# Other places for the last raw weight pieces, an earlier first layer, and VectorE alone for the inverse's copy and the turns of the state

## The chip, the cores and the metric

One core of a Trainium2 chip. The metric is the device time of one execution in microseconds (us). A run is the median of some executions. Ratios are the mean time of one kernel's fast runs over the mean time of the other's fast runs of the same rounds, so they are not quite the ratio of the medians that are quoted beside them. "Faster" or "slower" needs 2%.

One profile is one execution, and profiles scatter.

## The reference

Two layers one behind the other: a linear recurrence over 768 steps for 4 x 8 heads of width 40, then a feed-forward block on its output.

```python
def _attn_ref(r, k, v, w, a, b):              # each (4, 8, 768, 40)
    state = np.zeros((B, H, D, D))
    for t in range(S):
        y[:, :, t] = np.einsum('bhd,bhde->bhe', rt, state)
        Sa = np.einsum('bhde,bhe->bhd', state, at)
        state_decay = state * wt[:, :, None, :] - np.einsum('bhd,bhe->bhde', Sa, bt)
        state = state_decay + np.einsum('bhd,bhe->bhde', vt, kt)

def _moe_ref(x, w_in, w_out):                 # x (3072, 320), w_in (320, 2048), w_out (2048, 320)
    h = x @ w_in
    g = h * (1.0 / (1.0 + np.exp(-h)))
    return (g @ w_out)
```

The weights come as raw 64-bit numbers and are turned into fp32 on the chip.

## The kernel before

The recurrence runs in 12 chunks of 64 steps. A chunk needs the inverse of a triangular matrix per head. VectorE computes the inverses row by row (31 rows for a pair of chunks; for chunks 0 to 3 only 15 rows of half the size, and TensorE completes them with small products, `corners` and `complete`, in the "merge"). The inverse goes through DRAM (`mi`, `xd`, `XT`) to change its layout. From chunk 4 on, everything comes in pairs of chunks.

The feed-forward block of two finished chunks is cut into steps that fill TensorE's gaps: first-layer steps F (`ph`, then Silu on ScalarE into `gts`) and output steps S (`po<-wo_s,gts`, 16 matmul records each). Steps keep their order among themselves; against everything else the framework orders the queue of each engine by when it expects things to be ready, unless an order is laid down with `behind`. Each engine works its queue in order.

The raw weights arrive in pieces. A piece waits for a free place, is loaded there, and is converted by five VectorE and three ScalarE operations:

```python
def load_weights(done):
    while len(rooms) < NW:
        n = len(rooms)
        if n < NW // 2:
            place = ("wi0", "wi1", "wo0", "wo1", "room")[n % 5]
        elif n < NW * 3 // 4:
            place = ("wo0", "wo1", "room")[(n - NW // 2) % 3]
        else:
            place = ("mi", "tmp", "room")[(n - NW // 2) % 3]
        if taken.get(place, -1) > done:
            return
        ...

def weights(n, pin=lambda x: x, more=True):     # first half of piece n, second half of piece n-1
    if n < NW:
        pin(nc.vector.tensor_scalar(out=e, in0=hi, ...)); pin(nc.vector.tensor_scalar(out=f, in0=hi, ...))
        nc.scalar.activation(out=e, ...); nc.scalar.activation(out=f, ...); nc.scalar.activation(out=lo, ...)
    ...
    pin(nc.vector.scalar_tensor_tensor(...)); pin(nc.vector.tensor_tensor(...))
    pin(nc.vector.tensor_tensor(out=pieces[n][0], in0=f, in1=e, op=ALU.mult))
    if more: load_weights(n)

def in_order(x, line="moe"):                    # keeps the F and S steps in order
    if line in issued: behind(x, issued[line])
    issued[line] = x.ins
...
box["qq"] = sb.tile([128, N, 48], F32, name="qq", tag="tmp" if n > 0 else "xt")   # in merge()
...
def back():                                     # end of an inverse
    turned = XI.rearrange("p t s -> p s t")
    nc.scalar.copy(out=mi[L, 0:16], in_=turned[L, 0:16])
    pin(nc.vector.tensor_copy(out=mi[L, 16:32], in_=turned[L, 16:32]))
    send(queue, xd[L], mi[L])
...
for n in range(2, 4):                           # chunks 2 and 3
    ...
    now = {2: 4, 3: 5}[n]
    x = prepare(n + 2)
    if n == 2:
        weave(steps[0:4], queue[0:1], [x[i] for i in (0, 5, 1, 6)], convert[31:34])
    ...
    weave(steps[4:6] + late.pop(n, []) + ..., queue[1:now], scores + rows[0:36],
          convert[34:] if n == 2 else [])
```

## Time and profile before

901.05 us. In the profile (span 899.2 us) I use these places in time. They are read from the order of time on VectorE and TensorE. In the lines of profiles PE is TensorE's matmuls, PEld its weight loads, DVE VectorE, ACT ScalarE, POOL GpSimd and SPq the queue in which SyncE issues transfers; L825 is line 825 of that kernel. "Cold" means a granted TensorE clock of 0.50, "warm" one of 1.00.

| us from the start | kernel before |
|---|---|
| rows of the inverse of chunks 2 and 3 | 193.1 to 205.6 |
| qq of the merge of chunk 2, of chunk 3 | 220.6, 247.2 |
| first row of chunk 5 (inverse of chunks 4 and 5) | 310.0 |
| end of the rows of chunks 5, 7, 9, 11 | 349.3, 474.3, 597.8, 720.2 |
| the three later pairs together | 370.9 |
| last row to the end ("tail") | 179.0 |

Read it as three sums: the front up to the rows of chunk 5, three pairs, the tail. A change is worth what it does to each of the three.

### The profile page before, as it was taken

How to read it: one execution, taken by the hardware profiler on the slowest of the kernel's cores; microseconds unless marked ns; L12 is line 12 of the kernel's file. 1: busy time of each engine (PE TensorE's matmuls, PEld its weight loads, DVE VectorE, ACT ScalarE, POOL GpSimd, SP SyncE). 2: the span in 40 equal slices, each digit the busy share in tenths (PEclk: the TensorE clock that was granted, in tenths of full speed). 3: DMA queues.
4: the chain of work that ended last, by engine and by line, in shares of the span. 5: the costliest groups of instructions: out<-in, count | busy, mean ns of one | idle time of the engine just before them, and what ended most of it. 6: DMA issues, size and time to landing. Idle time of an engine off the chain costs nothing.

```text
span 899.2 us, 25358 instructions
## 1 busy us (share of the span) xinstructions
PE 778.9 (87%) x10914; PEld 552.9 (61%) x10914; DVE 557.9 (62%) x1084; ACT 297.4 (33%) x689; POOL 151.4 (17%) x156
## 2 busy tenths in 40 slices
PE   2145689896898997999998999999999989999995
PEld 2135677674786853875746857648757468574643
DVE  9979889885439598176896295982768912510000
ACT  2234358532622322514025342226140243311120
POOL 7312024200202201303102240113031000000001
PEclk9999869996759998999999999999999999999998
DMA  7875646744325542444613627325424021102001
GB/s 154 167 147 142 150 130 150 166 106 107 90 59 128 105 110 47 115 108 87 145 34 62 157 64 158 93 48 117 96 56 122 16 61 40 42 23 57 1 1 33
DMA packets 240151, 82.99 MB, mean 92 GB/s; under 512 B 207136, under 2 KB 231968, under 8 KB 240032
## 3 DMA queue, kind: packets, MB, share of 16 engines
q1 hardware_dynamic: 219488, 69.96, 34.8%
q10 hardware_dynamic: 20544, 11.34, 4.7%
q8 instruction: 87, 1.43, 0.7%
q14 instruction: 32, 0.26, 0.1%
HBM read 67.11 MB, written 14.16 MB: 90 GB/s over the span
## 4 chain that ended last, share of the span: by engine, by line
PE 45%; DVE 19%; DMA 3%; SPq 2%; issue 1%; ACT 1%; POOL 0%; POOLq 0%; ACTq 0%; DVEq 0%
PE po L825 14%; PE ph L813 9%; DVE tmp L419 7%; DVE XI L426 7%; PE pgy L264 4%; PE pl L264 3%; PE ph L818 3%; PE pm L264 2%; SPq L217 2%; PE pt L264 2%; PE pr L264 2%; PE po L264 2%; PE pq L264 2%; PE pu L264 2%; DVE GV L761 1%
## 5 line engine op out<-in xcount | busy, mean ns | idle before, releaser
L825 PE MATMUL po<-wo_s,gts 128*128 128x320 f32 x768 | 224.8, 448 | 17.1 <-ACT gts L820 10.8
L825 PEld LDWEIGHTS po<-wo_s,gts 128*128 128x128 f32 x768 | 145.2, 194 | 82.7 <-ACT gts L820 14.7
L813 PE MATMUL ph<-xt,wi_s 128*128 128x512 f32 (+1 forms) x448 | 182.2, 549 | 2.2 <-ACT ot L834 1.4
L813 PEld LDWEIGHTS ph<-xt,wi_s 128*128 128x128 f32 x448 | 82.1, 192 | 82.3 <-issue 67.9
L820 ACT ACTIVATE gts<-ph 128x512 f32<-128x512 f32 (+1 forms) x112 | 54.6, 531 | 161.1 <-PE ph L818 160.4
L722 DVE TENSOR_TENSOR vl<-pl,ml 128x512 f32<-128x512 f32 x48 | 30.9, 685 | 113.0 <-PE pl L264 77.6
L419 DVE TENSOR_TENSOR tmp<-XI,mi 64x2 f32<-64x2 f32 (+40 forms) x169 | 85.5, 506 | 8.8 <-DMA mi<-md 3.9
L841 POOL TENSOR_TENSOR ot<-gts,ot 128x320 f32<-128x320 f32 x24 | 21.8, 907 | 358.1 <-ACT gts L839 352.9
L336 DVE RECIPROCAL w<-W 128x512 f32<-128x512 f32 x24 | 80.3, 3347 | 1.3
L426 DVE TENSOR_REDUCE XI<-tmp 64x2 f32<-64x2 f32 (+40 forms) x169 | 77.0, 455 | 5.2
L264 PE MATMUL pq<-XT,sb 32*32 32x32 f32 (+1 forms) x1280 | 34.9, 207 | 32.6 <-DVE XT L463 21.1
L818 PE MATMUL ph<-xt,wl_s 64*128 64x512 f32 (+1 forms) x224 | 56.9, 585 | 0.0
L264 PE MATMUL pm<-a,kb 64*64 64x64 f32 x1280 | 41.5, 244 | 16.9 <-POOL kb L366 15.5
L264 PEld LDWEIGHTS pq<-XT,sb 32*32 32x32 f32 (+1 forms) x1280 | 31.6, 131 | 38.7 <-issue 16.0
L363 POOL TENSOR_TENSOR a<-a,W 64x512 f32<-64x512 f32 x32 | 39.5, 1236 | 75.4 <-DMA a<-in_aT 52.2
L1084 DVE TENSOR_SCALAR bad<-pb 1x1 int32<-1x1 f32 x1 | 0.1, 147 | 83.4 <-PE pb L1083 83.4
L264 PEld LDWEIGHTS pm<-a,kb 64*64 64x64 f32 x1280 | 38.1, 156 | 21.2 <-POOL kb L366 15.7
L839 ACT COPY gts<-po 128x320 f32<-128x320 f32 x24 | 10.2, 425 | 121.8 <-PE po L825 98.0
L264 PEld LDWEIGHTS pl<-r,vut 64*128 64x128 f32 x768 | 45.4, 189 | 4.7 <-ACT vl L650 2.1
L264 PE MATMUL pl<-r,vut 64*128 64x64 f32 x768 | 46.5, 274 | 2.0 <-ACT vl L650 2.0
L264 PE MATMUL pt<-ident,kb 128*128 128x128 f32 x192 | 29.1, 313 | 21.2 <-DVE a L308 21.2
L348 POOL TENSOR_TENSOR kb<-kb,w 128x512 f32<-128x512 f32 x20 | 24.8, 1238 | 131.9 <-DVE w L336 118.6
(108 smaller groups left out, 1060.7 us busy)
## 6 DMA issues: line engine op xcount, KB each, us to landing
kb<-in_bT SPq DMA_DIRECT2D x48, 128.0 KB
vut<-in_vT SPq DMA_DIRECT2D x48, 128.0 KB
r<-in_rT SPq DMA_DIRECT2D x24, 256.0 KB
w<-in_wT SPq DMA_DIRECT2D x45, 128.0 KB
kb<-in_kT SPq DMA_DIRECT2D x44, 128.0 KB
a<-in_aT SPq DMA_DIRECT2D x32, 128.0 KB
vl<-in_v SPq DMA_DIRECT2D x48, 80.0 KB
xs<-yx ACTq DMA_DIRECT2D x48, 80.0 KB
```

Source lines behind the costliest of these rows:

```text
L264: x = what(*x, **y)
L336: pin(nc.vector.reciprocal(R, u.W[:, :, 1 : C + 1]))
L348: nc.gpsimd.tensor_tensor(out=u.kb[:, :, 1], in0=u.kb[:, :, 1], in1=R, op=ALU.mult)
L363: nc.gpsimd.tensor_tensor(out=u.a[J, j], in0=u.a[J, j], in1=u.W[J, :, 0:C], op=ALU.mult)
L419: x = nc.vector.tensor_tensor(out=part, in0=X[L, :, t + 1 : N, t + 1 : N], in1=M[L, :, t, t + 1 : N].unsqueeze(2).to_broadcast([hi - lo, I ...
L426: x = nc.vector.tensor_reduce(out=X[L, :, t + 1 : N, t], in_=part, axis=AX.X, op=ALU.add)
L722: nc.vector.tensor_tensor(out=u.vl[:, :, j, D:], in0=pl[j].rearrange("p (q t) -> p q t", q=Q), in1=ml.unsqueeze(1).to_broadcast([128, Q, C ...
L813: in_order(nc.tensor.matmul(ph[n], lhsT=wi_s[:, k, at : at + 128], rhs=xt[:, k, :], start=k == 0, stop=False))
L818: in_order(nc.tensor.matmul(ph[n], lhsT=wl_s[R, i, :], rhs=xt[R, 2, :], start=False, stop=True))
L820: nc.scalar.activation(out=place(2 * i + n)[:, T], in_=ph[n], func=AF.Silu)
L825: in_order(nc.tensor.matmul(po[:, 0:DM], lhsT=place(f)[:, b * 128 : b * 128 + 128], rhs=wo_s[:, NF // 2 * half + f, :], start=f == 0, stop ...
L841: nc.gpsimd.tensor_tensor(out=ot4, in0=rest, in1=ot4, op=ALU.add)
```

## The change

Its intent: a raw piece in `tmp`, the buffer of qq, waits for the merge, the next merge's qq waits for that piece, and the output steps wait for the weights. So the last pieces get other places, buffers of chunk 1's keys that are free early; all first-layer steps of the last part come before its output steps; one step more is taken ahead of chunk 4. Besides, VectorE alone copies the inverse from chunk 4 on, and the turns of the state for odd chunks go from TensorE to VectorE.

```diff
-            elif n < NW * 3 // 4:
+            elif n < NW // 2 + 9:
                 place = ("wo0", "wo1", "room")[(n - NW // 2) % 3]
+            elif n == NW // 2 + 12:
+                place = "wo1"
             else:
-                place = ("mi", "tmp", "room")[(n - NW // 2) % 3]
+                place = ("room", "kb2", "kb3")[(n - NW // 2 - (8 if n < NW // 2 + 12 else 9)) % 3]
...
-            u.kb = sb.tile([128, Q, 2, C], F32, name="kb", bufs=6)
+            u.kb = sb.tile([128, Q, 2, C], F32, name="kb", tag=f"kb{(NM * u.n + u.m) % 6}")
...
-            nc.scalar.copy(out=mi[L, 0:16], in_=turned[L, 0:16])
-            pin(nc.vector.tensor_copy(out=mi[L, 16:32], in_=turned[L, 16:32]))
+            at = 0
+            if N == 16:
+                at = 16
+                nc.scalar.copy(out=mi[L, 0:16], in_=turned[L, 0:16])
+            x = nc.vector.tensor_copy(out=mi[L, at:32], in_=turned[L, at:32])
...
-            if u.n > 1 and u.n % 2 == 0:          # turns on VectorE
+            if u.n > 1 and u.n != 3:
...                                               # (odd ones held behind the next merge's transposes)
         for half in range(2):
+            sums = []
             for c in range(2 if apart else 1):
                 steps += [partial(first, T, NF // 4 * half + i) for i in range(NF // 4)]
-                steps += [partial(second, half, b) for b in range(T.start // 128, T.stop // 128)]
+                sums += [partial(second, half, b) for b in range(T.start // 128, T.stop // 128)]
+                if half == 0 or c > 0 or not apart:
+                    steps += sums
+                    sums = []
...
-        for u in units[n + 2]:
+        for u in units[n + 2] if n == 3 else []:
             load(u)
...
-        now = {2: 4, 3: 5}[n]
+        now = {2: 6, 3: 4}[n]
...
-            weave(steps[0:4], queue[0:1], [x[i] for i in (0, 5, 1, 6)], convert[31:34])
-            scores = [x[i] for i in (2, 4, 7, 9, 3, 8)]
+            weave(steps[0:4], queue[0:1], convert[31:])
+            scores = [partial(load, u) for u in units[n + 2]] + [x[i] for i in (0, 5, 1, 6, 2, 4, 7, 9, 3, 8)]
...
-            convert[34:] if n == 2 else [],
```

## The prediction

> **What bounds the kernel now.** I read four views in this order: busy time by stretch, the chain of work that ended last, the order of time on TensorE and VectorE, and what the DMA queue waited for. Stretches first (columns: us, then busy us and count of PE, PEld, DVE, ACT, POOL, then granted TensorE clock, DMA share, GB/s):
>
> ```profile
> 206.00:217.00 11.00, 4.42 (x13) 1.98 (x12) 4.70 (x13) 4.03 (x11) 0.00 (x0) 0.72 0.78 193
> 217.00:237.00 20.00, 16.84 (x529) 15.67 (x528) 8.46 (x19) 7.82 (x17) 1.04 (x2) 0.56 0.20 53
> 237.00:272.00 35.00, 31.35 (x866) 27.17 (x864) 14.20 (x33) 12.80 (x33) 6.15 (x6) 0.71 0.35 79
> ...
> 357.00:430.00 73.00, 72.56 (x1224) 53.81 (x1225) 38.20 (x64) 28.76 (x67) 16.88 (x16) 0.97 0.49 105
> 430.00:474.00 44.00, 42.99 (x359) 25.64 (x358) 40.69 (x83) 6.79 (x13) 3.88 (x4) 1.00 0.33 79
> 474.00:482.00 8.00, 6.05 (x16) 3.85 (x16) 6.11 (x6) 3.88 (x8) 2.32 (x2) 0.79 0.46 112
> ...
> 800.00:889.00 89.00, 88.89 (x386) 50.69 (x381) 1.58 (x5) 13.12 (x27) 5.97 (x7) 1.00 0.10 26
> ```
>
> There are three regimes. From about 357 us on, a pair of chunks is a loop of some 123 us (its inverse ends at 349, 474, 598 and 720 us): stage A of about 73 us, TensorE full; stage B of about 44 us, where VectorE computes 31 rows of the inverse one after another (DVE 40.7 of 44); then 8 us in which the inverse goes through DRAM. After 728 us TensorE alone works to the end. Before 310 us neither is full: between 206 and 272 us TensorE has gaps, and its granted clock is 0.56 to 0.72. That is the part which the change aims at, so next the order of time on TensorE there (start, us, what, idle time before and its releaser):
>
> ```profile
> 210.78 1.41 PE L825 MATMUL po<-wo_s,gts 128*128 128x320 f32 x2 [2.03 <-ACT gts L820]
> 215.88 1.44 PE L825 MATMUL po<-wo_s,gts 128*128 128x320 f32 x2 [3.68 <-DVE wo_s L190]
> ...
> 243.78 0.81 PE L825 MATMUL po<-wo_s,gts 128*128 128x320 f32 x2
> 247.17 2.50 PE L825 MATMUL po<-wo_s,gts 128*128 128x320 f32 x4 [2.58 <-DVE wo_s L190]
> ```
>
> The output layer's matmuls (L825) wait for pieces of wo_s that are still being converted. They stand in order before the merge of chunk 3's inverse and before the read of chunk 2, so the recurrence waits too. Why the pieces are late stands in the DMA queue's own waits between 185 and 275 us (total, times, longest):
>
> ```profile
> SPq L217 <- PE po L264: 22.2, 2, 11.3
> SPq L217 <- DVE wo_s L190: 14.8, 4, 6.0
> ```
>
> The last ten raw pieces take turns in "mi", "tmp" and "room". "tmp" is also the buffer of qq, which the merge's matmuls (po L264) read: a raw piece waits there for the merge, and the next merge's qq waits for that piece. On VectorE, in the same stretch:
>
> ```profile
> 246.36 0.75 DVE L190 TENSOR_TENSOR wo_s<-room 128x256 f32<-128x256 f32 x2
> 247.15 0.48 DVE L484 TENSOR_SCALAR qq<-pq,lower 128x256 f32<-128x256 f32 x1
> ```
>
> The merge's first product was done at 243.1 us, but qq comes only at 247.15, right behind the conversion.
>
> **What the Trainium skill says.** (1) "TensorE: Matmul & The Clock Gate", Part 1: TensorE falls to half clock after an idle window of some 3.4 us and recovers after as long a busy time. The trace agrees: in stretches of 4 us the granted clock is 0.50 from 212 to 232 us and from 248 to 264 us, behind the gaps above. (2) "VectorE: DVE Perf Modes", the tier table: an fp32 copy can run at two elements a cycle. The trace doesn't show that for the turned copy of the inverse (L436): 512 elements take 604 ns, about one per cycle at the page's 0.96 GHz, as the row products do (961 elements, 1160 ns). So I charge the full copy of 1024 at that slope. (3) "DMA: Bandwidth & Descriptors", Anatomy of one DMA: about 2 us fixed per transfer, mostly completion. The chain agrees: xd<-mi 2.64 us, XT<-xd 2.23 us; nothing in the change shortens these. (4) "Perfetto Trace Analysis", Optimization Strategy: repeated bubbles can mean that the next tile has no room. That is the case of "tmp" here.
>
> **Part 1, the pieces.** Pieces 29 and on go to kb2, kb3 and room (one to wo1). kb2 and kb3 held the keys of chunk 1 and are free by 161 us (before, chunk 4's keys load into them from then on), so raw data can be fetched during the inverse of chunks 2 and 3 (193 to 206 us) and the circle through qq is gone. The price is that chunk 4's keys load after the conversions instead of at 161 to 172 us; its scores are wanted only with chunk 5's (sent at 299 us). The conversions cost the same: 1.8 us of VectorE each (0.29+0.29+0.42+0.42+0.42). The four first-layer steps of the second token half now come before any second-layer step, so TensorE has two of them (2 x 2.65 us) for the hole at 208 to 217, and no output matmul stands between the merges.
>
> Gain, from TensorE's order between 237 and 272 us: the stall before 247.17 with the cold x4 behind it (243.78+0.81=244.6 to 249.6) is 5.0 us, the x2 at 253.2 is 1.4 us, and the merge, key and score matmuls to 265 us run cold. Cold against warm, from this trace: x61 of pq 3.2 against 1.26; x61 of po about 2.6 against 1.26; x96 of pm 4.46 against 3.0; the complete step about 3.5 against 2.4. That is 1.9+1.3+1.5+1.1=5.8 us. Together 12 us. The stretch 217 to 237 could save a further 5 us if it ran warm, but nine idle us before it shrink only to about four; I book 2. Against it, conversions whose data now come earlier can slip between the rows at 193 to 206, as three did before at 1.8 us each. I charge 2 to 3 such, 4 us, and half a us for waits elsewhere. Net: 12+2-4.5 = about -10 us at the start of chunk 5's rows (310 us before).
>
> **Part 2, one piece of second-layer work earlier.** Before chunk 4 ten steps of that queue are taken instead of nine. The backlog in every pair, and so in the last stretch where TensorE alone works, is one step less: 16 matmul records, 4.5 us (728 to 889 us is TensorE-bound). -4.5 us.
>
> **Part 3, the copy of the inverse.** Removed: ACT L435, 1.07 us, behind the last row. Added: VectorE copies all 1024 elements there, 0.07+1024x1.04 ns = 1.14 us, but its half copy in the middle of the rows (0.60 us) goes. The inverse leaves 0.5 us sooner, four times: -2 us. ScalarE no longer stands waiting (7.4 us at 349) in front of the last activations. The trace of the second pair shows what that blocked:
>
> ```profile
> 468.23 3.70 PE L813 MATMUL ph<-xt,wi_s 128*128 128x512 f32 x8
> 471.86 1.13 PE L818 MATMUL ph<-xt,wl_s 64*128 64x512 f32 x4
> 475.95 6.26 PE L825 MATMUL po<-wo_s,gts 128*128 128x320 f32 x16 [2.96 <-ACT gts L820]
> ```
>
> But the step at 475.95 lies in the 8 us in which the inverse is under way. Freed, it moves up into stage B; TensorE then stands idle until the inverse comes, 4 to 5 us, and the merge runs cold. Pair 1 shows that pattern already: from the last row's end to the end of pr 15.75 us, against 14.2 us in pairs 2 and 3. So +1.5 us twice: +3 us. Part 3 is +1 us in all.
>
> **Part 4, the turns of chunks 5, 7, 9.** Removed from stage B: per chunk 64 matmul records (2.0 us) and four ScalarE copies (0.58 us each). Added on VectorE in the next stage A: 16 transposes of 0.435 us, 7.0 us. They lie between the merge's transposes and the read (idle there 18.5 us in pair 1, 17 in pair 3), before the write needs them. Neither side is on the path: 0.
>
> **Sum.** 901 - 10 - 4.5 + 1 = about 887; some chance that the cold clock of 217 to 237 goes as well (up to -3 more) brings my figure to **885 us**.
>
> **The rivals.** (a) The whole front gain arrives: invert(3) isn't lengthened and both cold stretches go. For it: VectorE is busy only 27 of the 66 us between 206 and 272. Against: TensorE's queue is in order and the merges have short waits of their own. Then 872 to 878 us. (b) The wait is only replaced: kb of chunk 4 or its a (which waits for pr at 236 us) becomes the late transfer, or chunk 4's scaling, 2 x 4.7 us of VectorE, stands before a qq. Against: the scores have some 30 us to spare. The front then gives 2 us, and the tail stays: 893 to 896. (c) VectorE becomes the bound in stage A through the extra transposes. For: every vl waits in its queue behind them. Against: DVE is 38 of 73 us there. It would cost up to 7 us in three pairs, about 900. (d) The later pairs get worse by the cold clock than I book, 2 to 3 us in each: 890 to 895.
>
> **Range and chances.** The tail's 4.5 us are nearly sure; the front is 2 to 20 us, wide because a queue order that I cannot see decides it. The 80% range is 874 to 897. Two per cent faster is 883.0, a little below my figure, so faster 0.40, same 0.57, slower 0.03.
>
> **What would show it.** Right: no L825 wait for wo_s L190 between 206 and 272; no DMA-queue wait on po L264 of that size; chunk 5's rows start near 300 us; clock in 240 to 272 near 1; the last row-to-end time (720 to 899 before, 179 us) about 4 to 5 us shorter; idle TensorE of 4 to 5 us before each merge; GT transposes 128 instead of 80 and no vl waiting on them. Wrong: rows of chunk 5 still at 307 to 310 us with another releaser, or pairs longer than 123 us.

## The result, and the profile after

The changed kernel takes **907.97 us** (906.57 to 909.49, four runs) against 900.75; the ratio is 1.0077, 95% interval 1.0054 to 1.0101. That is within 2%, but it is slower by 7 us where 16 us less was predicted, and outside the range.

| us | before | after | difference | predicted |
|---|---|---|---|---|
| rows of the inverse of chunks 2 and 3 | 193.1 to 205.6 | 194.8 to 211.9 | end +6.3 | +4 |
| qq of chunk 2, of chunk 3 | 220.6, 247.2 | 229.4, 254.7 | +8.8, +7.5 | |
| first row of chunk 5 | 310.0 | 324.3 | **+14.3** | **-10** |
| end of chunk 5's rows | 349.3 | 361.9 | +12.6 | -10 |
| three pairs | 370.9 | 372.8 | +1.9 | +1 |
| tail | 179.0 | 170.6 | -8.4 | -4.5 |
| span of the profile | 899.2 | 905.3 | +6.1 | |

So the loss is in the front. First the stretches, in the columns of the prediction (us, then busy us and count of PE, PEld, DVE, ACT, POOL, then granted clock, DMA share, GB/s):

```profile
206.00:217.00 11.00, 7.86 (x29) 4.77 (x30) 6.31 (x10) 2.67 (x7) 2.48 (x2) 0.80 0.53 152
217.00:237.00 20.00, 17.14 (x368) 11.57 (x367) 6.53 (x11) 2.59 (x8) 1.04 (x2) 0.93 0.16 26
237.00:272.00 35.00, 32.01 (x823) 25.56 (x824) 1.74 (x4) 15.21 (x35) 6.58 (x7) 0.65 0.26 60
```

The hole at 206 to 217 is filled (7.86 us of TensorE against 4.42) and 217 to 237 runs nearly warm (0.93 against 0.56), as hoped. But in 217 to 237 TensorE issued 368 records and not 529: it is busy with large ones that are not the merge. The order of time on TensorE says which (start, us, what, idle time before and its releaser):

```profile
213.35 2.08 PE L825 MATMUL ph<-xt,wi_s 128*128 128x256 f32 x4 [3.14 <-ACT gts L832]
...
226.88 1.34 PE L837 MATMUL po<-wo_s,gts 128*128 128x320 f32 x4
229.29 1.34 PE L837 MATMUL po<-wo_s,gts 128*128 128x320 f32 x4
...
235.70 1.81 PE L837 MATMUL po<-wo_s,gts 128*128 128x320 f32 x4
...
239.28 2.50 PE L837 MATMUL po<-wo_s,gts 128*128 128x320 f32 x4
```

The first-layer steps go on until 226.9 us, and then output matmuls stand before and between the merge's products. None of them waits for weights any more; that wait is gone, as predicted. The wait had kept them behind the recurrence, and now nothing does. On the chain of work that ended last, from qq of chunk 2 to the first row of chunk 5, output matmuls (L837) take 13.5%, some 12.8 of 95 us. The queue is then empty where the kernel before still had two output steps and first-layer steps to do: under chunk 5's rows, between 325 and 345 us, TensorE is busy 10.2 of 20 us (20.0 before).

The other thing is on VectorE, during the rows of the inverse of chunks 2 and 3:

```profile
194.40 0.43 DVE L193 TENSOR_TENSOR room<-room 128x256 f32<-128x256 f32 x1
194.75 0.16 DVE L423 TENSOR_TENSOR tmp<-XI,mi 128x2 f32<-128x2 f32 x1
...
196.43 0.17 DVE L423 TENSOR_TENSOR tmp<-XI,mi 128x18 f32<-128x18 f32 x1
196.51 0.29 DVE L182 TENSOR_SCALAR room<-room 128x256 int32<-128x256 int32 x1
196.72 0.17 DVE L430 TENSOR_REDUCE XI<-tmp 128x6 f32<-128x18 f32 x1
196.80 0.28 DVE L183 TENSOR_SCALAR room<-room 128x256 int32<-128x256 int32 x1
```

Conversions (L182 to L194) alternate with the rows (L423, L430). Between 189 and 200 us there are 26 of them, 9.6 us, against 10 and 3.7 us before. What the DMA queue waited for, 185 to 275 us (total, times, longest), answers to the prediction's view; the wait on po is gone. The longest wait is a new one, for the first output rows (`ot`); no transfer stands on the chain of work named above, so it wasn't on the path:

```profile
SPq L857 <- POOL ot L853: 23.5, 1, 23.5
SPq L221 <- DVE wo_s L194: 10.2, 8, 2.2
```

My first theory after this result was the **order**: the wait for weights had been a brake, and without it independent work runs ahead of the recurrence. Its rivals were the **conversions** in the rows, and the late parts. The experiments show that both the order and the conversions count. Why the stall that I had seen was worth so little is shown in part (a second engine waited beside it); that the supply of instructions takes back some of the rest is partly argued.

### The profile page after: what moved, and what is told of

Its sections match the earlier page's. It is cut to its first block, busy times and chain, and to the rows that moved or that the text cites. A ratio compares the mean times of both kernels' runs of the same rounds, so it can differ in the third digit from the quotient of the medians.

```text
span 905.3 us, 24996 instructions
## 1 busy us (share of the span) xinstructions
PE 778.4 (86%) x10722; PEld 546.8 (60%) x10722; DVE 580.1 (64%) x1132; ACT 285.4 (32%) x673; POOL 150.1 (17%) x156
## 3 DMA queue, kind: packets, MB, share of 16 engines
q8 instruction: 86, 1.41, 0.7%
## 4 chain that ended last, share of the span: by engine, by line
PE 56%; DVE 28%; DMA 8%; issue 3%; SPq 3%; ACT 2%; POOL 1%; ACTq 0%; POOLq 0%; DVEq 0%
PE po L837 13%; PE ph L825 13%; DVE tmp L423 7%; DVE XI L430 6%; PE pgy L268 4%; PE pl L268 4%; PE ph L830 4%; PE po L268 3%; PE pt L268 3%; PE pq L268 3%; SPq L221 3%; PE pu L268 2%; DVE w L340 2%; PE pr L268 2%; PE pm L268 2%
## 5 line engine op out<-in xcount | busy, mean ns | idle before, releaser
L837 PE MATMUL po<-wo_s,gts 128*128 128x320 f32 x768 | 221.6, 444 | 1.5 <-issue 1.5
L825 PE MATMUL ph<-xt,wi_s 128*128 128x512 f32 (+1 forms) x448 | 191.4, 571 | 21.9 <-DMA xt<-xs 15.6
L837 PEld LDWEIGHTS po<-wo_s,gts 128*128 128x128 f32 x768 | 144.3, 192 | 64.0 <-issue 7.8
L825 PEld LDWEIGHTS ph<-xt,wi_s 128*128 128x128 f32 x448 | 85.3, 201 | 108.2 <-issue 81.0
L423 DVE TENSOR_TENSOR tmp<-XI,mi 64x2 f32<-64x2 f32 (+40 forms) x169 | 84.6, 500 | 10.5 <-DMA mi<-md 5.9
L430 DVE TENSOR_REDUCE XI<-tmp 64x2 f32<-64x2 f32 (+40 forms) x169 | 76.8, 455 | 4.9
L696 DVE STREAM_TRANSPOSE GT<-GV 32x256 f32<-32x256 f32 x128 | 55.7, 435 | 8.1 <-DMA GV<-in_v 6.0
L268 PE MATMUL pq<-XT,sb 32*32 32x32 f32 (+1 forms) x1280 | 31.4, 204 | 31.2 <-DVE XT L472 20.5
L268 PE MATMUL pm<-a,kb 64*64 64x64 f32 x1280 | 39.6, 235 | 17.7 <-POOL kb L370 15.5
L268 PEld LDWEIGHTS pq<-XT,sb 32*32 32x32 f32 (+1 forms) x1280 | 28.2, 126 | 38.4 <-issue 15.5
L851 ACT COPY gts<-po 128x320 f32<-128x320 f32 x24 | 10.2, 424 | 126.6 <-PE po L837 98.6
```

The lines of the kernel that those rows point to most:

```text
L268: x = what(*x, **y)
L423: x = nc.vector.tensor_tensor(out=part, in0=X[L, :, t + 1 : N, t + 1 : N], in1=M[L, :, t, t + 1 : N].unsqueeze(2).to_broadcast([hi - lo, I ...
L430: x = nc.vector.tensor_reduce(out=X[L, :, t + 1 : N, t], in_=part, axis=AX.X, op=ALU.add)
L696: x = nc.vector.transpose(out=gt[T, :, 32 * e : 32 * e + 32], in_=wide[E, at : at + Q * D].rearrange("p (q d) -> p q d", q=Q)[:, :, 0:32],)
L825: in_order(nc.tensor.matmul(ph[n], lhsT=wi_s[:, k, at : at + 128], rhs=xt[:, k, :], start=k == 0, stop=False))
L837: in_order(nc.tensor.matmul(po[:, 0:DM], lhsT=place(f)[:, b * 128 : b * 128 + 128], rhs=wo_s[:, NF // 2 * half + f, :], start=f == 0, stop ...
```

## The experiments

All are compared with the kernel before in the same rounds; the table gives them all. All outputs are right. "Rows 5" is the first row of chunk 5.

| run | what | us, median (range) | ratio to before (95%) | rows 5 | pairs | tail |
|---|---|---|---|---|---|---|
| e1_late | before + copy and turns on VectorE | 906.66 (903.12 to 908.15) | 1.0040 (1.0004 to 1.0076) | 309.0 | 374.9 | 178.9 |
| e2_front | before + places + step order | 908.39 (904.87 to 911.65) | 1.0051 (1.0003 to 1.0099) | 326.5 | 371.8 | 170.8 |
| e3_places | before + places | 913.69 (909.28 to 917.15) | 1.0116 (1.0062 to 1.0170) | 321.0 | 375.4 | 175.4 |
| e4_steps | before + step order | 904.23 (902.03 to 906.25) | 1.0001 (0.9960 to 1.0042) | 320.9 | 371.6 | 172.7 |
| e5_rows | after, conversions held | 895.18 (889.66 to 900.43) | 0.9912 (0.9837 to 0.9987) | 310.7 | 371.0 | 173.4 |
| e6_hold | after, steps held | 900.14 (897.35 to 902.55) | 0.9975 (0.9918 to 1.0031) | 316.2 | 370.2 | 170.5 |
| e7_both | after, both held | 893.57 (892.17 to 894.93) | 0.9898 (0.9843 to 0.9953) | 306.4 | 375.1 | 170.5 |
| e8_hold_before | before, output steps held | 903.09 (897.90 to 904.17) | 0.9979 (0.9918 to 1.0040) | 308.7 | 375.9 | 177.4 |
| e9_twice | e7, one product twice | 898.83 (896.40 to 904.16) | 0.9970 (0.9919 to 1.0020) | 316.6 | 369.2 | 172.0 |
| e10_notmp | e8, no piece in tmp | 900.52 (897.45 to 902.12) | 0.9970 (0.9929 to 1.0011) | 307.9 | 372.2 | 177.9 |
| e11_front_held | e7 without the late parts | 890.25 (886.50 to 898.14) | 0.9878 (0.9811 to 0.9944) | 305.6 | 372.4 | 171.0 |
| e12_warm | e7, extra matmuls | 898.01 (891.35 to 903.77) | 0.9967 (0.9920 to 1.0014) | 310.0 | 367.5 | 173.5 |

The kernel before took 904.15, 901.31 and 901.80 us in the three sets of rounds.

**The change in parts.** The diff falls into four groups: places with the loads and conversions that belong to them, step order with `now`, the copy of the inverse, the turns. Four kernels take one or two groups each; their edits are the hunks above.

> Only the two late parts: VectorE alone copies the inverse (chunks 4 and on), and VectorE turns the state of chunks 5, 7, 9 in the next pair. Pieces and steps as before. Theory 1 (the loss is all in the front: dense-layer steps now stand in TensorE's in-order queue ahead of the merges of chunks 2 and 3, and conversions stand between the rows of their inverse): front unchanged, chunk 5's rows start at 310 +-1 us, pairs within 2 us of before, total 898 to 903. Rival 2 (the late parts cost the time: extra VectorE work delays the reads, or the cold clock after the idle gap): front unchanged but each pair 2 us longer, total 905 or more.

> Only the front parts: new places of the raw pieces with their conversion order, and the new order and number of dense-layer steps. Theory 1: chunk 5's rows start at about 324 us as in the changed kernel, the stretch after the last inverse is shorter than before's 179 us by 4 to 9, total 904 to 909. Rival 2: about 896 to 900.

> Only the new places of the raw pieces (with kb2 and kb3, the later load of chunk 4 and the earlier conversions); steps of the dense layer as before. The built order already shows the output matmuls and most of the second token half's first-layer matmuls ahead of or within the merge of chunk 2. Theory 1a (the wait for wo_s was a brake that kept these out of the way; pieces alone cause the loss): rows of chunk 5 at 318 to 324 us, tail as before, total 907 to 914. Theory 1b (the step order causes it): rows of chunk 5 at or before 310 us, total 893 to 901.

> Only the new order and number of dense-layer steps (all first-layer steps of the second weight half before its output steps, six and four steps taken instead of four and five); raw pieces in their old places. Theory 1a: the wait for wo_s stays, the rows of inverse 2/3 keep their old length, chunk 5's rows at 310 to 314 us, tail 4 to 5 us shorter, total 897 to 901. Theory 1b: rows of chunk 5 at 318 us or later, total 903 or more.

The late parts alone leave the front where it was (rows 5 at 309.0, before 310.0), so the front's loss isn't theirs. The time of e1, 906.66 us, missed the theory's 898 to 903 all the same and lies where its rival put it (905 or more); what that comes from is taken up at e11. Places alone delay rows 5 by 11.0 us, the step order alone by 10.9, both together by 16.5, the whole change by 14.3. So e3 went to theory 1a and e4 to 1b: each of the two is bad by itself, they are not additive, and the whole gain that there is lies in the tail. In e4 the conversions are those of the kernel before, and the inverse's rows last 12.5 us as there; there it is the order alone: from the end of the rows to qq of chunk 2 it takes 19.1 us, 15.1 in the kernel before and 14.9 in e1. (Its rows begin at 195.8, as in e1, 195.3, so some 2 of the 10.9 us are scatter.)

**Conversions held (e5_rows).** The changed kernel, with late conversions on VectorE ordered behind the last row:

```diff
             mark["row"] = x.ins
+            if lo == 0 and hi == 128 and N == 16:
+                mark["turned"] = x.ins            # rows of the inverse of chunks 2 and 3
...
+    for n in range(31, NW + 1):
+        convert[n] = partial(weights, n, lambda x: behind(x, mark["turned"]))
```

> The changed kernel, with the conversions of pieces 31 and later ordered behind the last row of the inverse of chunks 2 and 3 on VectorE (an order on one engine, no new wait); nothing else is touched. Theory (two causes: the conversions lengthen the rows by 4.7 us, and TensorE's freed steps stand before and between the merge's matmuls): the rows take 12.5 us again and not 17.2, the corner product of chunk 2's merge comes 3 to 5 us earlier than in the changed kernel (224 to 226 against 229.4), and the rows of chunk 5 start at 317 to 321 (324.3 in the changed kernel, 310.0 in the kernel before), so that most of the delay stays; 901 to 905 us against the kernel before's 901. Rival (the conversions between the rows are the whole delay, the matmul order does nothing): rows of chunk 5 start at 308 to 311, and the time is 892 to 895.

This went to the rival. Rows 5 start at 310.7, 13.7 us earlier than in the changed kernel, and the time is 895.18. My theory had left only 3 to 7 us for the conversions. Here is the order of time on VectorE in this kernel, the first and the last row:

```profile
189.03 0.17 DVE L423 TENSOR_TENSOR tmp<-XI,mi 128x2 f32<-128x2 f32 x1 [1.93 <-DMA mi<-md]
...
199.30 0.62 DVE L430 TENSOR_REDUCE XI<-tmp 128x30 f32<-128x450 f32 x1
199.84 0.28 DVE L182 TENSOR_SCALAR room<-room 128x256 int32<-128x256 int32 x1
```

The rows last 10.9 us, not 17.2, and they begin at 189.0, not 194.8, which I had not looked at. Here the first row waits for nothing but its data, the last load `mi<-md`. The order of time in SyncE's queue says when that was issued, in the changed kernel and in this one:

```profile
182.27 1.94 SPq L221 DMA_DIRECT2D md<-sb  x4
187.99 2.46 SPq L221 DMA_DIRECT2D room<-in_w_out  x3
190.63 0.48 SPq L221 DMA_DIRECT2D mi<-md  x1
```

```profile
182.02 1.94 SPq L221 DMA_DIRECT2D md<-sb  x4
184.34 0.35 SPq L221 DMA_DIRECT2D room<-in_w_out  x1
185.67 0.48 SPq L221 DMA_DIRECT2D mi<-md  x1
```

In the changed kernel three loads of raw pieces stand ahead of it, which themselves wait for conversions to end (the first for 3.7 us), and it leaves 5.0 us later. In VectorE's own queue conversions stand ahead of the first row too, but only until 194.75; in e5 the load took 3.3 us, so it can hardly have landed before 194.0 (an estimate from 190.63 and 3.3). So the conversions delay the start mainly through SyncE's queue. The inverse ends 12.0 us earlier, and rows 5 follow by 13.7. The F steps still stand among the first products of the merge: from the end of the inverse to rows 5 it takes 110.7 us, little less than in the changed kernel (112.4), so nearly all of the gain is the inverse's.

**Steps held (e6_hold) and both (e7_both).** Two orders on TensorE: the fifth of the last first-layer steps not before the merge of chunk 2 is complete, the first output step not before that of chunk 3. e7 adds the edit of e5.

```diff
+    hold = []
     def in_order(x, line="moe"):
+        if line == "moe" and hold:
+            behind(x, hold.pop())
...
-                    product(                      # last product of merge n
+                    mark[f"merged{n}"] = product(
...
+    def held_step(step, name):
+        hold.append(mark[name])
+        step()
+    queue[4] = partial(held_step, queue[4], "merged2")
+    queue[8] = partial(held_step, queue[8], "merged3")
```

> The changed kernel, with two orders on TensorE alone: the fifth first-layer step of the last part of chunks 0 and 1 not before the merge of chunk 2 is complete, the first output step not before the merge of chunk 3 is complete. Theory (the freed steps ran ahead of the recurrence): the corner product of chunk 2's merge comes 4 to 6 us earlier (224 to 226), that of chunk 3 at 243 to 248 (254.7 in the changed kernel), the rows of chunk 5 start at 309 to 315, and the time is 892 to 898, so 0.3 to 1% below the kernel before. Rival (the delay comes from the longer rows and the later conversions alone, or from the late parts of the change): the rows of chunk 5 start at 320 or later and the time stays within 2 us of 908. Third possibility: a TensorE with less to do between the merge's matmuls runs at half clock more often, and the gain is only half: 315 to 319.

> The changed kernel with the orders of both other runs: the late conversions behind the rows of the inverse of chunks 2 and 3, and the steps held behind the two merges. Theory: the two causes add up. Rows 12.5 us, corner products at 219 to 222 and 238 to 243, rows of chunk 5 at 303 to 309 (310.0 in the kernel before), rows of the later pairs as before, tail about 171 us; so 886 to 893, below both kernels by about 1%. If the steps held back leave TensorE cold or are only moved under chunk 5's rows where they lengthen something, it is 895 to 900.

e6: rows 5 at 316.2, 8.1 us earlier than in the changed kernel although the rows of the inverse are as long as there (17.4 us). So the order counts as well. It came out at the third possibility of the text, half of the gain, and 900.14 us. e7: 306.4, which is 18.0 us earlier than the changed kernel and 3.6 earlier than the kernel before; 893.57 us, just above the expected 886 to 893. The two holds bring 13.7 and 8.1 us alone and 18.0 together: both causes are shown, and they share some 4 us.

**The stall by itself (e8_hold_before, e10_notmp).** If the two causes are taken away, the front should gain the 12 us of stall and cold clock that the prediction counted. It gains 3.6, and this is the inverse's: in e7 it ends 5.2 us earlier than in the kernel before, which has conversions of its own between and ahead of the rows. Behind the inverse e7 takes 106.0 us to rows 5, the kernel before 104.4. (The kernel before with the conversions held, and nothing of the change, was not run; it may gain as much.) So the stall is tested in the kernel before, without any of the change: e8 holds the first output step, which stood waiting for weights between the merges, behind the merge of chunk 3; e10 also keeps the pieces out of `tmp`.

```diff
+    queue[4] = partial(held_step, queue[4], "merged3")          # e8 and e10
...
-                place = ("mi", "tmp", "room")[(n - NW // 2) % 3]
+                place = ("mi", "room")[n % 2]                    # e10
```

> The kernel before with one order on TensorE alone: the first output step of the last part, which in the kernel before stood in TensorE's queue waiting for the second half of the output weights between the two merges, not before the merge of chunk 3 is complete. Nothing of the change is in it. It tells what the stall cost by itself: if the 12 us of waiting that the prediction counted was on the path, the corner product of chunk 3 comes at 235 to 241 (247.2 in the kernel before) and the rows of chunk 5 start at 299 to 304, so 890 to 896. If the wait was only filled time before the next thing ready, the rows start at 307 to 311 and the time is 899 to 902.

> The kernel before with the output steps held behind the merge of chunk 3 (as in the earlier run) and, besides, the last raw pieces in two places, mi and room, instead of three, so that none lies in tmp, the buffer of qq. Nothing else of the change is in it. In the run with the hold alone qq of chunk 3 came right behind a conversion on VectorE at 248.85, 4.5 us after its product was done. Theory (the conversion of the piece in tmp was the real wait in front of qq, and TensorE's wait for the weights only ran beside it): qq of chunk 3 comes at 243 to 246, right behind its product, and the rows of chunk 5 start at 304 to 307 (310.0 before, 308.7 with the hold alone). Since the small matmuls behind it then have no wait in front of them, the supply of instructions takes 1 to 2 us of that back. 896 to 900 us. Rival (the wait before qq covered time that something else needs anyway): rows of chunk 5 at 308 to 310, 900 to 903. The output weights come later with two places; that may delay the output steps, which stand under chunk 5's rows and cost nothing there.

e8: TensorE's wait for the weights is gone, and nothing is won: rows 5 at 308.7, 903.09 us. VectorE and TensorE at that place:

```profile
248.18 0.75 DVE L190 TENSOR_TENSOR wo_s<-room 128x256 f32<-128x256 f32 x2
248.85 0.47 DVE L488 TENSOR_SCALAR qq<-pq,lower 128x256 f32<-128x256 f32 x1
```

```profile
249.58 0.22 PE L268 MATMUL po<-XT,qq 32*16 32x16 f32 x5 [4.13 <-DVE qq L488]
...
254.16 0.20 PE L268 MATMUL po<-XT,qq 32*16 32x16 f32 x2 [2.28 <-issue]
```

qq still comes right behind the conversion. The wait of TensorE for the weights ran beside VectorE's work on the same pieces, which stands ahead of qq in VectorE's queue, and only the longer of two parallel waits costs. The prediction showed that very pair of lines and yet booked the stall on TensorE. e10 takes the second wait away too: qq of chunk 3 comes 0.7 us after its product's end. From the end of the inverse's rows to rows 5 it is 98.8 us, against 104.4 in the kernel before, 101.0 in e1 and 101.7 in e8, so some 2 to 6 us are won behind the inverse. But the inverse itself ends 3.5 us later than before in this profile (2.5 later in e1), so rows 5 come at 307.9 and the time is 900.52, not separable from the kernel before. The expectation of 304 to 307 was missed by 1 us.

**The supply of instructions (e9_twice).** The second fence above has a wait of 2.28 us "<-issue", in the midst of a product, and such waits stand in many merges: time in which TensorE waits for nothing that the profile shows. (Not in every one, as the expectation of e9 below says: the merges of chunks 2 and 3 in the kernel before have none over 0.81 us.) They come after runs of 128 records. In the run with both holds:

```profile
242.46 0.21 PE L272 MATMUL po<-XT,qq 32*16 32x16 f32 x2 [1.80 <-issue]
...
246.46 0.22 PE L272 MATMUL po<-XT,qq 32*16 32x16 f32 x5 [2.09 <-issue]
```

Between the two lie 128 records, which ran from 242.46 to 244.37, and then nothing for 2.09 us. In the run they took 15 ns each, so it is no pace of the single record that limits them. The Trainium skill, "Runtime: NRT & Kernel Launch", Instruction fetch mechanics, says that an engine's instructions are fetched while it runs, in blocks of 256 instructions (16 KiB). 128 records with their weight loads are 256 instructions, and the profile's DMA queues show the fetches, here for the run with both holds (packets, MB, share):

```profile
q8 instruction: 86, 1.41, 0.7%
```

1.41 MB in 86 packets is 16.4 KB each. In the run with both holds one such packet starts in each of the windows 239.9 to 240.3, 243.4 to 243.8 and 247.4 to 247.8 us, and none in the 3.1 and 3.6 us between. So a block takes about 4 us when TensorE is hungry. The traces here have fifteen runs of 128 records up to chunk 5 that lie between two such waits of 0.8 us or more. From start to start they took 3.46 to 4.83 us, seven of them 3.97 to 4.00: 27 to 38 ns a record. The page calls the cost of crossing a block "mostly hidden"; for these small matmuls the measurement says otherwise. To test it, the first product of the merges of chunks 2 and 3 (128 records) is issued twice, with the same result:

```diff
-            for h in range(N):
+            for h in [*range(N), *range(N)] if n > 1 else range(N):
                 for r in range(0, 128, 32):       # corners(), first product
```

> The kernel with both holds, with the first product of the merges of chunks 2 and 3 (128 small matmul records, pq) issued twice with the same result, to ask what limits the small matmuls of the merge. Theory (the supply of instructions: in every merge so far TensorE stood for 1.8 to 3.1 us with nothing to wait for, always after a run of 128 matmul records, and one such run takes 3.4 to 4.5 us from its start to the start of the next): 128 more records cost 3.5 to 4 us in each merge, so the rows of chunk 5 start 6 to 8 us later than with both holds alone (306.4), at 312.5 to 314.5, and the time is 899 to 902. Rival (the clock and the array limit them, 10 to 15 ns a record, as the prediction charged): 1.3 to 1.9 us in each merge, rows of chunk 5 at 309 to 310.3.

```profile
241.89 2.11 PE L272 MATMUL pq<-XT,sb 16*32 16x16 f32 x187
246.31 1.15 PE L272 MATMUL pq<-XT,sb 16*32 16x16 f32 x69 [2.30 <-issue]
```

In chunk 3's merge the product takes 5.6 us (241.89 to 247.46) against 1.4, in chunk 2's 5.1 against 1.9. Rows 5 come 10.2 us later. The rival said 3 to 4 us, the theory 6 to 8. The two products themselves grew by 7.4 us, and a wait again stands in the midst of one, so this went to the theory; the other 2.8 us are of the size of the scatter. That the fetch makes the wait, and not another thing that comes every 256 instructions, rests on the times of the packets and was not tested by itself. In e7 such waits (3.9 us) and first-layer steps (4.3 us) stand on the chain behind qq of chunk 3.

With this the merge of chunk 2 in the kernel before can be read again: its four products are 448 records, and the last 442 of them ran from 218.69 to 231.99, 13.3 us or 30 ns each. It ran at about the pace of the supply while the clock was at half. This is an estimate from the rates above and not shown by a run of its own.

**Warm from the start (e12_warm).** Twelve useless matmuls while the inverse is in DRAM, so that the merge begins at full clock:

```diff
+            if n == 2:
+                junk = bank("pq")
+                for i in range(12):
+                    x = nc.tensor.matmul(junk, lhsT=wi_s[:, 0, 0:128],
+                                         rhs=mark["tiles"][0][:, 0:512], start=True, stop=True)
...                                               # (each behind the one before)
```

> Both holds, and twelve extra matmuls without use (128x512, about 0.46 us each at full clock) on TensorE in the way of the inverse of chunks 2 and 3 through DRAM, about 202 to 208 us, so that the merge of chunk 2 starts at full clock and not at half. The prediction charged the cold clock 5.8 us in such a merge. Clock theory: from qq of chunk 2 to the end of its pr 17 us cold (214.5 to 231.6 with both holds), 11 to 12 us warm, rows of chunk 5 at 300 to 302, 885 to 889 us. Supply theory: the 320 small records take as long warm as cold, only the larger pt and pr matmuls gain (6.5 us cold, some 4 warm): 14.5 to 16 us, rows of chunk 5 at 304 to 306, 891 to 894 us.

Neither number came. I had taken 0.46 us for a matmul of this size; each is two records, and they took 10.6 us, to 212.5. Two first-layer steps thereby fell into the merge. From qq to the end of pr it is 19.0 us, not 11 to 16, and rows 5 come at 310.0. As a test of warm against cold it is spoilt by that. One thing is clear in it, though, in narrow stretches:

```profile
217.00:218.00 1.00, 0.26 (x23) 0.15 (x12) 0.75 (x2) 0.06 (x1) 0.00 (x0) 1.00 0.00 0
218.00:219.00 1.00, 0.52 (x42) 0.52 (x43) 0.00 (x0) 0.00 (x0) 0.00 (x0) 0.73 0.00 0
219.00:220.00 1.00, 1.00 (x88) 1.00 (x81) 0.00 (x0) 0.00 (x0) 0.00 (x0) 0.50 0.07 16
```

The clock goes from 1.00 to 0.50 in the middle of the merge, though TensorE's longest gap there is 1.22 us. Warming it beforehand didn't hold here.

**The best version (e11_front_held).** Both holds, places and step order, without the late parts; the edits are those of e5 and e6 on top of e2.

> Both holds as before, but with the places and the step order of the change alone: the copy of the inverse and the turns of the state are as in the kernel before. It tells what these two late parts are worth beside the mended front, and whether this is the best version. Front as with both holds: rows of chunk 5 at 305 to 308. In the run of the late parts alone the three later pairs were together 3.9 us longer than in the kernel before in the one profile (374.8 against 370.9), about what the prediction booked (1 to 3 us), and with both holds 375.2. If that is theirs, the pairs here take 371 to 372 and the time is 889 to 892; if it is scatter between runs, 374 to 376 and 892 to 895.

890.25 us, ratio 0.9878 (0.9811 to 0.9944). It beats the kernel before by 1.2% and the changed one by about 2% (its ratio over 1.0077, from different rounds). Rows 5 at 305.6, tail 171.0. Whether the late parts cost anything is not settled by it: the three pairs took 372.4 us here and 375.1 in e7, but over all profiles they took 367.5 to 375.1 with the late parts (seven kernels, mean 371.5) and 370.9 to 375.9 without (seven, mean 372.9). The scatter of the profiles is larger than any effect, and e7 and e11 have overlapping ranges. The one sign against the late parts is the time of e1, 0.4% above the kernel before (interval 1.0004 to 1.0076).

## Why the prediction was wrong

The step that failed is **Part 1**: "TensorE has two of them (2 x 2.65 us) for the hole at 208 to 217, and no output matmul stands between the merges", and the sum from it, "12+2-4.5 = about -10 us at the start of chunk 5's rows". It came out at +14.3. Three terms of it, each with its run:

1. **The stall, 6.4 us of the 12.** It did disappear: L837 waits for no weights between 206 and 272 us. It was worth nothing (e8: -1.3 us at rows 5, time unchanged), because qq waited beside it on VectorE for the same pieces. Without both waits some 2 to 6 us are won behind the inverse (e10), of which the runs show no gain in time.
2. **The cold clock, 5.8 us.** I took cold and warm durations of the merge's products and booked the difference. In the changed kernel the merge of chunk 2 did begin warm, and its `complete` product took 5.2 us, 230.56 to 235.77, against 3.8 us cold before; I had booked 2.4. Waits of 0.81 and 2.06 us "<-issue" stand in it, which e9 ties to the supply of instructions; that the supply caught up while the kernel before stood waiting is an explanation and not shown. So a warm clock alone did not bring the booked gain. What the prediction read from the clock was too simple as well: behind the wait of 2.58 us before 247.17 it stayed at half until 264, and from 212 to 232 it stayed at half although TensorE was busy 13.2 of those 20 us.
3. **The conversions, booked at +4 us.** The inverse ended 6.4 us later than in the kernel before, 4.7 of it in longer rows and 1.7 in a later start. Holding all late conversions, also those that the kernel before has there, brought rows 5 forward by 13.7 us (e5). I counted only conversions between the rows; the start of the rows hangs on a load that stands behind raw pieces in SyncE's queue (issued at 190.6 us, 188.4 before, 185.7 in e5). The charge of 1.8 us each was misread too: two conversions stand between the rows of the kernel before, and its rows lasted 1.6 us longer than e5's, which have none. The change moves all late conversions into the weave in front of chunk 2's rest, and with their data there early, nothing keeps them out of the rows.

And one term was missing: I wrote that no output matmul stands between the merges. I deduced it from the order of the steps among themselves, and nothing in the new text fixes their order against the merge. They ran ahead as soon as they could, which is 8.1 us (e6). The range's low confidence had its reason in the text itself, "a queue order that I cannot see decides it"; but the range still reached only to a front that gains 2 us, and none of the four rivals let the front lose.

**Part 2** was right in kind: -8.4 us in this profile against -4.5. The nine kernels with the change's step order have tails of 170.5 to 173.5 us, mean 171.7; the five with the old one 175.4 to 179.0, mean 177.7. So the step order is worth 6.0 us on average, of which 4.5 is the step that I counted. Where the other 1.5 us come from I leave open.

**Part 3 and 4** were right within the scatter. The copy of 1024 elements took 1.06 us (1.14 predicted). The turns became 128 transposes of 435 ns, up from 80, and rows and pairs didn't move. The idle TensorE of 4 to 5 us before each merge, which I expected, was there in e1 (5.3, 3.8 and 3.9 us) and only 0.6, 2.1 and 1.2 us in the changed kernel.

Of the rivals, (b), the wait is replaced, comes nearest, but it expected +2 us and not a loss.

## What to carry to other kernels

A wait in an in-order queue can be a brake that keeps filler work behind the critical chain; before you remove it, lay down what the freed work must stay behind. The two orders here, each within one engine's queue, turned a loss of 0.8% into a gain of 1.0 to 1.2%. Before booking a stall, look whether a second engine waits beside it for the same thing, and test the stall alone with one added order; and count the instructions of a stretch of small matmuls before hoping for a faster clock.

## What the Trainium skill lacked or had wrong

- "Runtime: NRT & Kernel Launch", Instruction fetch mechanics, calls the crossing of a 16 KiB block mostly hidden. TensorE stood 0.8 to 3.1 us in waits that go with such crossings in the merges, and one block of 128 small records with their weight loads took 3.46 to 4.83 us from start to start (27 to 38 ns a record).
- "TensorE: Matmul & The Clock Gate", Part 1, ties half clock to an idle window of about 3.4 us. In a stretch of small matmuls (16x16 to 32x32) the granted clock fell from 1.00 to 0.50 with a longest gap of 1.22 us (e12) and, in the changed kernel at 236 us, 2.06 us. The same part does say that frequent short idle times between groups of matmuls can bring half clock back, but gives no length for them, nor how small matmuls count as activity.
- "VectorE: DVE Perf Modes", the tier table, has an fp32 copy at two elements a cycle. The turned copy of the inverse took 0.60 us for 512 and 1.06 us for 1024 elements a partition, 0.90 ns an element from the one to the other; the table doesn't speak of reads with a stride (other pages of the skill do, without a rate for such a copy).
